# Eighty unread products behind the rounded exponentials of the first ten units

## The chip, the core and the metric

The kernel runs on one core of a Trainium2 chip. The time is that of one execution on the device, in microseconds; the kernel before took 715.68 us in the median of three runs (712.08 to 719.77).

## The reference

Attention with a bias that a small network makes of the distance, then a feed-forward layer, for 4 batches, 8 heads, 576 positions and head size 64:

```python
scores = q @ k.T / 8
x = log1p(|i - j|) / log1p(max(i, 1))
bias = relu(x * w1 + b1) @ w2            # 32 hidden, one value per head
attn = exp(s - max(s)) / (sum + 1e-9)    # s = scores + bias
x = (attn @ v) as 2304 x 512
h = x @ w_in                             # 512 -> 2048
out = (h * sigmoid(1.702 h)) @ w_out     # 2048 -> 512
```

## The kernel before

Numbers go through TensorE in fp16 as a high and a low half, so each product of two matrices is three (high by high, high by low, low by high). The work is cut into units: a unit is one batch, one tile of 128 query rows (the fifth tile of a batch has 64) and a pair of heads. There are 72 units, 36 for each group of two batches; units 0 to 7 belong to the first tile of batches 0 and 1. For a unit:

- `emit_s` (L346): twelve score products on TensorE into a PSUM tile that has one buffer, tag s.
- `emit_soft1` (L364): VectorE adds the bias and takes the maximum (L373), ScalarE takes the exponential and its sum (L377), VectorE makes the reciprocal (L384, L385), ScalarE (L389) or VectorE (L387) writes the rounded high half of the normalised exponentials into tile hl, VectorE the low half (L390), and a DMA on SP's queue transposes both (L399).
- `emit_av` (L405): thirty products with v (L422) into a PSUM tile of tag h, which VectorE scales and splits into xT (L427, L428).

The bias of a query tile comes from 8 bias steps of four relus each on ScalarE or VectorE (L172, L174), products with w2 on TensorE (L191, L193), a copy out by ScalarE (L197), a DMA to memory and a load (L212). The weights arrive in 32 pieces that VectorE puts together from 64-bit words (L464, L467, L470), and that ScalarE (L476) and VectorE (L226) split. When all 8 units of a block of rows are through, the feed-forward runs in 16 chunks per block: `emit_m1`, twelve products (L500) into tag h, a tanh (L506), VectorE (L508), a split (L513 or L515, L516), and two chunks later `emit_m2`, six products (L530).

Tag h has two PSUM buffers, which key transposes (L293, L300), attention products and feed-forward products take in the order of the program text. Key transposes for units 4 and 5 are called at unit 2, those for units 6 and 7 at unit 4; the attention products lag four units behind the scores for the first eight (`AV_LAG`). The main loop (L667) calls these pieces, but the order on each engine is made by a scheduler that plays the program through with its own costs and puts each instruction where it is ready. On the chip each engine then takes its instructions in that order.

Of the kernel before, what the change touches and what calls it, by code (L numbers as in the profile page):

```python
# [7 lines left out]
F32 = mybir.dt.float32  # L8
# [12 lines left out]
def kernel(  # L21
# [26 lines left out]
    nc = tc.nc  # L48
# [41 lines left out]
    ps_h = ctx.enter_context(tc.tile_pool(name="ps_h", bufs=2, space=PSUM))  # L90
# [128 lines left out]
    def stage(shape, dt, tag, name):  # L219
        return wk.tile(shape, dt, tag=tag, name=name, bufs=BUFS[tag])  # L220
# [143 lines left out]
    def emit_soft1(u):  # L364
        bt = bt_t[u]
        at = wk.tile([128, 2 * S], F32, tag="a32", name="a32", bufs=BUFS["a32"])
        mx = wk.tile([128, 2], F32, tag="mx", name="mx")
        sm = wk.tile([128, 2], F32, tag="sm", name="sm", bufs=6)
        hl = wk.tile([128, 2, 2 * S], F16, tag="hl", name="hl", bufs=BUFS["hl"])
        for a in range(2):  # L370
            cs = slice(S * a, S * a + S)

            nc.vector.tensor_tensor_reduce(  # L373
                out=at[:, cs], in0=s_ps.pop((u, a))[:, 0:S], in1=bt[:, cs], scale=-1.0 / BS, scalar=3.0e38,
                op0=ALU.add, op1=ALU.min, accum_out=mx[:, a:a + 1],
            )
            nc.scalar.activation(  # L377
                out=at[:, cs], in_=at[:, cs], func=ACTF.Exp, scale=-1.0, bias=mx[:, a:a + 1],
                accum_out=sm[:, a:a + 1],
            )  # L380
        for a in range(2):
            cs = slice(S * a, S * a + S)
            r = sm[:, a:a + 1]
            nc.vector.tensor_scalar(out=r, in0=r, scalar1=1.0e-9, scalar2=1.0 / AS, op0=ALU.add, op1=ALU.mult)  # L384
            nc.vector.reciprocal(out=r, in_=r)  # L385
            if a < VEC_EXP.get(u, 0):
                nc.vector.tensor_scalar(out=hl[:, 0, cs], in0=at[:, cs], scalar1=r, scalar2=None, op0=ALU.mult)  # L387
            else:
                nc.scalar.activation(out=hl[:, 0, cs], in_=at[:, cs], func=ACTF.Identity, scale=r)  # L389
            nc.vector.scalar_tensor_tensor(  # L390
                out=hl[:, 1, cs], in0=at[:, cs], scalar=r, in1=hl[:, 0, cs], op0=ALU.mult, op1=ALU.subtract
            )

        if u in AT_W:
            x = 8 * 2 * DM + 18 * 128 * AT_W[u]
            t = wo16.rearrange("p f x d -> p (f x d)")[:, x:x + 18 * 128].rearrange("p (c n) -> p c n", c=18)
        else:
            t = stage([128, 18, 128], F16, "aT" if u <= max(BIAS_A) or u % 4 < 2 else "ht", "aT")
        nc.sync.dma_start_transpose(out=t, in_=hl.rearrange("p x n -> p (x n)"))  # L399
        aT[u] = t  # L400
# [266 lines left out]
    for u in range(NU + 2):  # L667
        if u < NU:
            emit_s(u)
            emit_soft1(u)  # L670
        ready = NF * sum(1 for x in last_unit if x < av)
        late = u - AV_LAG.get(u, 2) in last_unit[1:]
        if not late:
            msteps(ready, STEPS_A.get(u, 1))
        while av <= u - AV_LAG.get(u, 2):
            emit_av(av)
            av += 1
        if late:
            msteps(ready, STEPS_A.get(u, 1))
        elif u - 2 == last_unit[0]:  # L680
            ready = NF
        if u < len(W_STEPS):
            weights_to(w_done[1] + W_STEPS[u])
        if u in BIAS_A:
            bias_first()
        msteps(ready, STEPS_B.get(u, 1))
        bias_second()
        if u in BIAS_B:
            bias_first()
            bias_second()  # L690
        if u + BIAS_AHEAD < NU:
            bias_get(u + BIAS_AHEAD)
        for fn, args in todo.get(u, ()):
            fn(*args)
# [56 lines left out]
```

## Time and profile before

| | before |
|---|---|
| runs | 712.08, 715.68, 719.77 us |
| profiled execution | 715.95 us, span 714.2 us |
| mean granted clock of TensorE | 0.956 |
| busy: TensorE, VectorE, ScalarE | 637.2, 510.9, 404.4 us |
| first score product, first feed-forward product | 30.5, 116.95 us |

Times in the trace run from the start of the span. Busy time of TensorE counts pipelined products, so a full row means that it had no pauses. The granted clock is 1.00 at 2.4 GHz and 0.50 at 1.2 GHz; a value between is a mean over a stretch.

### The profile page before, as it was taken

Reading aid. Unit: us, or ns where it says so; the run is one execution under the profiler, and the core shown is the slowest. Engines: PE = TensorE matmul, PEld = TensorE weight load, DVE = VectorE, ACT = ScalarE, POOL = GpSimd, SP = SyncE. Lnnn points to the kernel's source line nnn. Section 1 sums busy time; section 2 is a strip of 40 time slices with the busy share of each in tenths; the row PEclk is TensorE's granted clock in tenths of the full one; section 3 lists DMA queues with packets and bytes.
Section 4 is the critical chain, followed back from the end, with each engine's and each line's share of the span. In section 5 each row is a group of like instructions: output and inputs, shape, how many; then the busy total and the mean of one; then the engine's idle time right before and its main releaser. Section 6 shows DMA issues by size and latency. Waiting matters only on the chain. (4 is left out here: it accounts for less than half of the span.)

```text
span 714.2 us, 17518 instructions
## 1 busy us (share of the span) xinstructions
PE 637.2 (89%) x6888; PEld 385.7 (54%) x6888; DVE 510.9 (72%) x1401; ACT 404.4 (57%) x865; POOL 135.5 (19%) x198
## 2 busy tenths in 40 slices
PE   5656867798789999999789899799999999999997
PEld 3222423354445665566556565466656666666765
DVE  6678888999867778676569877746766896774321
ACT  6789987786757566554455547624334363443133
POOL 1202000112202211111212221111122222222222
PEclk9979896999989999999989999999999999999999
DMA  9799999999988675668875769844673585745000
GB/s 236 228 286 230 287 251 231 276 256 237 198 149 204 144 140 117 147 140 153 186 133 112 145 126 193 178 94 96 106 146 87 101 189 109 132 68 97 2 31 16
DMA packets 230770, 111.79 MB, mean 157 GB/s; under 512 B 210720, under 2 KB 214944, under 8 KB 230688
## 3 DMA queue, kind: packets, MB, share of 16 engines
q1 hardware_dynamic: 222592, 94.65, 64.0%
q10 hardware_dynamic: 7952, 15.43, 6.8%
q8 instruction: 54, 0.88, 0.5%
q0 software_dynamic: 144, 0.59, 0.2%
q14 instruction: 28, 0.23, 0.1%
HBM read 52.85 MB, written 15.34 MB: 95 GB/s over the span
## 5 line engine op out<-in xcount | busy, mean ns | idle before, releaser
L500 PE MATMUL hp<-xT,wi 128*128 128x256 f16 (+1 forms) x1920 | 217.1, 264 | 6.0 <-DVE th L508 4.9
L530 PE MATMUL op<-wo,gT 128*128 128x512 f16 x864 | 215.3, 383 | 2.7 <-POOL gT L516 1.3
L516 POOL TENSOR_TENSOR gT<-th,gT 128x256 f16<-128x256 f32 (+1 forms) x160 | 119.9, 751 | 502.1 <-ACT gT L513 221.6
L500 PEld LDWEIGHTS <-wi 128*128 128x128 f16 x1920 | 167.5, 98 | 49.8 <-issue 16.9
L377 ACT ACTIVATE a<-a,mx 128x576 f32<-128x576 f32 x144 | 110.3, 767 | 110.8 <-DVE mx L373 108.2
L390 DVE SCALAR_TENSOR_TENSOR hl<-a,sm,hl 128x576 f16<-128x576 f32 x144 | 122.4, 863 | 17.2 <-ACT hl L389 16.8
L373 DVE CUSTOM_DVE_ANT_0 a<-sp,bt 128x576 f32<-128x576 f32 x144 | 103.0, 753 | 35.8 <-PE sp L357 30.7
L530 PEld LDWEIGHTS <-gT 128*128 128x128 f16 x864 | 79.6, 98 | 81.6 <-POOL gT L516 4.9
L506 ACT ACTIVATE th<-hp 128x256 f32<-128x256 f32 (+1 forms) x160 | 56.2, 353 | 109.3 <-PE hp L500 104.6
L508 DVE SCALAR_TENSOR_TENSOR th<-th,hp 128x256 f32<-128x256 f32 (+1 forms) x160 | 62.2, 391 | 76.2 <-ACT th L506 76.1
L422 PEld LDWEIGHTS <-v 128*64 128x64 f16 x2400 | 69.6, 115 | 51.5 <-issue 29.7
L422 PE MATMUL ot<-aT,v 128*64 128x128 f16 (+1 forms) x2280 | 79.8, 222 | 19.2 <-DMA aT<-hl 15.3
L389 ACT ACTIVATE hl<-a,sm 128x576 f16<-128x576 f32 x103 | 76.2, 767 | 25.8 <-issue 10.8
L357 PE MATMUL sp<-kT,qT 64*128 64x512 f16 (+2 forms) x960 | 72.7, 293 | 12.0 <-DVE mx L373 6.3
L191 PE MATMUL o<-ht,pk 128*32 128x512 f32 x288 | 63.0, 693 | 20.9 <-ACT os L197 18.2
L172 ACT ACTIVATE ht<-tab,bp 128x576 f32<-128x576 f32 x96 | 69.3, 768 | 6.5 <-PE o L193 5.7
L357 PEld LDWEIGHTS <-qT 64*128 64x128 f16 (+1 forms) x960 | 29.4, 98 | 59.7 <-issue 29.3
L427 DVE TENSOR_SCALAR xT<-ot 128x128 f16<-128x128 f32 x72 | 20.4, 284 | 22.3 <-PE ot L422 22.0
L384 DVE TENSOR_SCALAR sm<-sm 128x1 f32<-128x1 f32 x144 | 21.5, 149 | 17.6 <-ACT a L377 16.5
L197 ACT ACTIVATE os<-o,ips 128x576 f32<-128x576 f32 x36 | 26.3, 731 | 12.1 <-PE o L193 11.5
L191 PEld LDWEIGHTS o<-ht,pk 128*32 128x32 f32 x288 | 10.2, 115 | 40.9 <-ACT os L197 21.1
L515 DVE CAST gT<-th 128x256 f16<-128x256 f32 x96 | 28.1, 293 | 3.6
(60 smaller groups left out, 439.8 us busy)
## 6 DMA issues: line engine op xcount, KB each, us to landing
bt<-scr SPq DMA_DIRECT2D x31, 576.0 KB, 4.4
scr<-os ACTq DMA_DIRECT2D x36, 288.0 KB, 4.6
w<-in_moe_w_in_dram SPq DMA_DIRECT2D x16, 512.0 KB, 5.5
w<-in_moe_w_out_dram SPq DMA_DIRECT2D x16, 512.0 KB, 5.3
k<-in_k_dram SPq DMA_DIRECT2D x32, 128.0 KB, 4.2
q<-in_q_dram SPq DMA_DIRECT2D x16, 256.0 KB, 5.0
out_dram<-ob ACTq DMA_DIRECT2D x16, 256.0 KB, 3.9
bt<-scr SPq DMA_DIRECT2D x8, 288.0 KB, 4.2
```

The lines of the kernel that those rows point to most:

```text
L172: last["A"] = nc.scalar.activation(out=h, in_=tv, func=ACTF.Relu, bias=bp[:, pb:pb + 1])
L191: nc.tensor.matmul(om[po], lhsT=w2b, rhs=h[:, :, 0:128], start=True, stop=True)
L357: nc.tensor.matmul(ps[a][64 * e:64 * e + m, cs], lhsT=qt[r, x, hp + e, 0:m], rhs=kT[b, hp + e][r, y, cs], start=i == 0, stop=i == 2,)
L373: nc.vector.tensor_tensor_reduce(out=at[:, cs], in0=s_ps.pop((u, a))[:, 0:S], in1=bt[:, cs], scale=-1.0 / BS, scalar=3.0e38, op0=ALU.add, ...
L377: nc.scalar.activation(out=at[:, cs], in_=at[:, cs], func=ACTF.Exp, scale=-1.0, bias=mx[:, a:a + 1], accum_out=sm[:, a:a + 1],)
L389: nc.scalar.activation(out=hl[:, 0, cs], in_=at[:, cs], func=ACTF.Identity, scale=r)
L390: nc.vector.scalar_tensor_tensor(out=hl[:, 1, cs], in0=at[:, cs], scalar=r, in1=hl[:, 0, cs], op0=ALU.mult, op1=ALU.subtract)
L422: nc.tensor.matmul(o[64 * a:64 * a + 64, po], lhsT=vt[:, x, vc:vc + 64], rhs=t[:, 9 * y + k0, po], start=kb < 0 and i == 0, stop=kb == 3 a ...
L500: nc.tensor.matmul(p[:, :n], lhsT=wi16[:, x, cc, 128 * f:128 * f + 128], rhs=r, start=i == 0, stop=i == 11,)
L508: nc.vector.scalar_tensor_tensor(out=g[:, :n], in0=th[:, :n], scalar=1.0, in1=p[:, :n], op0=ALU.add, op1=ALU.mult)
L516: nc.gpsimd.tensor_tensor(out=gt[:, 1, :n], in0=g[:, :n], in1=gt[:, 0, :n], op=ALU.subtract)
L530: nc.tensor.matmul(op_t[j, i], lhsT=gt[:, x, ts], rhs=wo16[:, f, y, :], start=f == 0 and n3 == 0, stop=f == NF - 1 and n3 == 2,)
```

## The change

Behind the rounding of each head in units 0 to 9, TensorE makes four equal products of 384 columns: the first 128 columns of that head's rounded exponentials stand still, the other columns stream. They go into a new tile of tag h that nothing reads.

```diff
             else:
                 nc.scalar.activation(out=hl[:, 0, cs], in_=at[:, cs], func=ACTF.Identity, scale=r)
+            if u < 10:
+                e = hl[:, 0, cs]
+                w = ps_h.tile([128, 512], F32, tag="h", name="wm")
+                for _ in range(4):
+                    nc.tensor.matmul(w[:, 0:384], lhsT=e[:, 0:128], rhs=e[:, 128:512], start=True, stop=True)
             nc.vector.scalar_tensor_tensor(
```

Lines behind it move down by five (L476 becomes L481, L500 becomes L505). The scheduler makes another order of everything from the first tens of rows on; TensorE has 12,582 rows instead of 12,420.

TensorE, the key transposes for units 4 and 5 (kt and kp of L293 and L300). Before, they stand between the first bias steps, ahead of all scores:

```order
L282 MATMUL kp<-idn,kt_99 128x64
L281 MATMUL kp<-idn,k_92 128x128 x4
L282 MATMUL kp<-idn,kt_99 128x64
L293 MATMUL kt<-idn,kt_99 128x64 x2
L191 MATMUL o<-ht,pk 32x512 x4
```

Now, row 182 on, behind the eight new products wm of unit 2:

```order
L394 LDWEIGHTS hl
L394 MATMUL wm<-hl 128x384
L293 MATMUL kt<-idn,kt_99 128x64 x2
L300 MATMUL kp<-idn,k_138 128x128 x4
L191 MATMUL o<-ht,pk 32x512 x4
L193 MATMUL o<-ht,pk 32x64 x4
```

The transposes have moved from ahead of unit 0 to behind the rounding of unit 2.

ScalarE, between the exponentials of unit 5 and those of unit 6 (a_825 and a_923 before, a_983 is unit 6 now). Before, all that stands between them:

```order
L377 ACTIVATE a_825,sm<-a_825,mx 128x576 x2
L172 ACTIVATE ht<-tab,bp 128x576
L197 ACTIVATE os<-o,ips 128x576
L172 ACTIVATE ht<-tab,bp 128x576 x3
L256 ACTIVATE qT<-qp 128x512
L377 ACTIVATE a_923,sm<-a_923,mx 128x576
```

Now, the last eleven of the sixteen rows between them, and the exponentials:

```order
L198 DMA scr_81<-os 128x576
L302 ACTIVATE kT<-kp 128x512
L172 ACTIVATE ht<-tab,bp 128x576
L197 ACTIVATE os<-o,ips 128x576
L172 ACTIVATE ht<-tab,bp 128x576 x3
L481 ACTIVATE wi_72<-w_1300 128x512
L302 ACTIVATE kT<-kp 128x512
L198 DMA scr_82<-os 128x576
L172 ACTIVATE ht<-tab,bp 128x576
L197 ACTIVATE os<-o,ips 128x576
L172 ACTIVATE ht<-tab,bp 128x576 x3
L377 ACTIVATE a_983,sm<-a_983,mx 128x576 x2
```

Bias steps and weights now stand around the copies of the late transposes, ahead of unit 6.

## Rows read from the trace of the kernel before

**Rows 1.** Stretch: length; busy us of PE, PEld, DVE, ACT, POOL; granted clock, DMA share, GB/s.

```profile
30.00:117.00 87.00, 57.60 (x559) 25.85 (x559) 72.87 (x181) 76.73 (x140) 5.41 (x6) 0.80 0.98 248
117.00:200.00 83.00, 68.58 (x667) 37.44 (x666) 74.77 (x178) 60.22 (x118) 13.91 (x14) 0.93 1.00 243
200.00:297.00 97.00, 96.16 (x1049) 57.72 (x1049) 72.75 (x205) 62.12 (x127) 18.77 (x23) 0.99 0.72 151
```

**Rows 2.** The same view, later stretches.

```profile
340.00:400.00 60.00, 50.11 (x622) 32.89 (x621) 44.57 (x124) 31.09 (x69) 11.72 (x19) 0.94 0.67 138
...
440.00:460.00 20.00, 15.72 (x213) 9.83 (x212) 15.87 (x55) 15.45 (x41) 2.48 (x6) 1.00 0.95 189
460.00:660.00 200.00, 199.22 (x2220) 126.39 (x2218) 137.81 (x404) 80.70 (x197) 46.16 (x57) 0.99 0.57 112
```

**Rows 3.** Who waited for whom, 30 to 117 us: total us, times, longest.

```profile
DVE xT L427 <- PE ot L422: 4.5, 2, 3.6
...
ACT ht L172 <- PE o L193: 3.1, 3, 2.5
```

**Rows 4.** Busy time by stretch, two short ones in the head.

```profile
45.00:51.00 6.00, 5.01 (x28) 1.99 (x28) 5.34 (x12) 5.95 (x12) 0.00 (x0) 0.50 1.03 256
61.00:62.50 1.50, 1.08 (x14) 0.51 (x16) 1.50 (x5) 1.50 (x3) 0.00 (x0) 1.00 0.85 276
```

**Rows 5.** Order of time: start us, us, engine, line, [idle before]; products that begin or wait.

```profile
116.95 1.25 PE L500 MATMUL hp<-xT,wi 128*128 128x256 f16 x5
...
198.11 1.81 PE L422 MATMUL ot<-aT,v 128*64 128x128 f16 x30 [5.64 <-DMA aT<-hl]
...
297.44 1.48 PE L500 MATMUL hp<-xT,wi 128*128 128x256 f16 x12
```

**Rows 6.** The chain that ended last: start us, us, what; twelve first feed-forward products.

```profile
667.66 1.31 PE hp L500 x12
```

**Rows 7.** Order of time: the score products of units 2 and 4.

```profile
49.35 1.62 PE L357 MATMUL sp<-kT,qT 64*128 64x512 f16 x12
...
61.11 0.91 PE L357 MATMUL sp<-kT,qT 64*128 64x512 f16 x12 [0.82 <-DVE mx L373]
```

**Rows 8.** Groups by line, 30 to 117 us: count, busy us, mean ns, idle before.

```profile
L172 ACT ACTIVATE ht<-tab,bp 128x576 f32<-128x576 f32 x46 | 33.2, 768 | 3.2 <-PE o L193 3.1
...
L197 ACT ACTIVATE os<-o,ips 128x576 f32<-128x576 f32 x12 | 8.7, 725 | 0.0
...
L389 ACT ACTIVATE hl<-a,sm 128x576 f16<-128x576 f32 x14 | 10.3, 765 | 1.6 <-DVE sm L385 1.0 <-DMA aT<-hl 0.6
...
L476 ACT ACTIVATE wi<-w 128x512 f16<-128x512 f32 x8 | 4.9, 624 | 2.5 <-DVE w L470 2.4
...
L226 DVE SCALAR_TENSOR_TENSOR wi<-w,wi 128x512 f16<-128x512 f32 x8 | 5.4, 681 | 0.0
...
L373 DVE CUSTOM_DVE_ANT_0 a<-sp,bt 128x576 f32<-128x576 f32 x20 | 14.3, 751 | 5.0 <-DMA bt<-scr 5.0
...
L384 DVE TENSOR_SCALAR sm<-sm 128x1 f32<-128x1 f32 x18 | 2.6, 145 | 1.6 <-ACT a L377 1.5
...
L387 DVE TENSOR_SCALAR hl<-a,sm 128x576 f16<-128x576 f32 x4 | 2.0, 504 | 0.0
...
L390 DVE SCALAR_TENSOR_TENSOR hl<-a,sm,hl 128x576 f16<-128x576 f32 x18 | 14.3, 809 | 1.2 <-ACT hl L389 1.2
...
L464 DVE TENSOR_SCALAR w<-w 128x512 uint32<-128x512 uint32 x15 | 6.2, 416 | 0.6 <-DMA w<-in_moe_w_in_dram 0.4
...
L467 DVE SCALAR_TENSOR_TENSOR w<-w,w 128x512 uint32<-128x512 uint32 x15 | 10.2, 686 | 0.1
...
L470 DVE SCALAR_TENSOR_TENSOR w<-w,w 128x512 uint32<-128x512 uint32 x14 | 10.3, 736 | 0.0
```

**Rows 9.** Groups by line, 117 to 200 us: the bias products.

```profile
L191 PE MATMUL o<-ht,pk 128*32 128x512 f32 x64 | 12.5, 625 | 1.7 <-DVE mx L373 1.7
...
L193 PE MATMUL o<-ht,pk 128*32 128x64 f32 x64 | 4.2, 282 | 0.0
```

## The prediction

> **What bounds the kernel now.** I read first the busy time by stretch [rows 1]. From 117 us on, when the first feed-forward product runs, TensorE is the engine that fills the time: 96.16 us busy of 97 between 200 and 297 us, and nearly all of it again from 460 to 660 us [rows 2]. Before 117 us it is not: between 30 and 117 us TensorE works 57.60 of 87 us, while VectorE works 72.87 and ScalarE 76.73. In that head the two softmax engines set the pace and TensorE waits. The waits say the same [rows 3]: there ScalarE waited for bias products 3.1 us and VectorE for attention outputs 4.5 us, and no more than that for anything TensorE makes. The clock granted to TensorE in the head is 0.80 of full on average; the stretches at 0.50 lie in its pauses and bias steps [rows 1, 4].
>
> So an end time has three parts: when the first feed-forward product can start, the TensorE work from there on, and the pauses inside that work. The change touches the order up to one place only. TensorE's rows are the same in both programs from row 3,697 of before (3,859 of the changed one) on; what stands there in the trace is the second half of the attention products that ends where a feed-forward chunk begins at 297.44 us [rows 5]. VectorE, ScalarE and the DMA queue of SP also run in one order from about there. I therefore reckon up to 297 us, and let the rest (417 us) stay as it is, with its pauses of 9.9 us in 340 to 400 and 4.3 us in 440 to 460 [rows 2].
>
> In the trace that stretch is 117.0 + 164.7 + 15.3 = 297.0: start of the first product at 116.95 [rows 5], 68.58 + 96.16 us of TensorE work, 14.4 + 0.8 us of pauses [rows 1].
>
> **The change, part by part.**
>
> *The products themselves.* 10 units by 2 heads by 4 are 80 products of 384 columns. Twelve products of 256 columns take 1.31 us at full clock [rows 6], 109 ns each, so 384 columns take 164 ns and all 80 take 13.1 us; the twelve score products, which take 0.91 us at the full clock, take 1.62 at half [rows 4, 7], so at half clock at most 26.2 us. The weight load that each carries lies under the product before it, as in the 1.31 us. All 80 stand ahead of the first feed-forward product, in a stretch with 29.4 us of TensorE pauses (87 minus 57.6) that the softmax engines make. I cost them at nothing as work. If that cover were gone (TensorE the pace setter of the head), 13.1 us would be added.
>
> *The waits they bring.* TensorE takes its products in order, so the four of a head hold all behind them until ScalarE has rounded that head. They also take their turn in the two accumulators with tag h, by program order. Before, the key transposes that units 4 and 5 need ran from row 10 of TensorE on; now they stand behind the products of unit 2, and the attention products of unit 0 stand behind those of unit 4. So those units' scores come late, and the scheduler filled ScalarE and VectorE with other work ahead of them. Counted in the orders, ScalarE now does ahead of unit 6's exponentials 16 more bias relus, 4 more bias copies, 2 more weight halves and one copy of queries less: 16 x 0.768 + 4 x 0.725 + 2 x 0.624 - 0.6 = 15.8 us [rows 8]. Nothing of it is new work: by unit 10's exponentials, ScalarE's count is about that of before.
>
> *The start of the feed-forward.* It needs the attention output of unit 7 from VectorE. Ahead of that copy VectorE's order now has 8 more low halves of weights, two more score passes, 8 more small operations, 2 more low halves of exponentials, and 7, 7 and 6 more of the three steps that put weights together: 5.4 + 1.5 + 1.2 + 1.6 + 2.9 + 4.8 + 4.4 = 21.8 us [rows 8]. ScalarE has ahead of the first tanh 8 more relus, 2 copies, 4 passes of the exponentials and 7 weight halves: 6.1 + 1.5 + 3.1 + 4.4 = 15.1 us, the exponential taken at the price of the rounding [rows 8]. With the pauses as they are the start moves by 15.1 to 21.8 us; VectorE's 14.1 us of pauses in the head [rows 1] could take up part, the new waits could add some. I take 18 us, the middle, since both engines must get there: 135 us.
>
> *The work behind the start.* Two units of scores (0.91 us each) and three bias steps now stand ahead of it. Eight bias steps cost 12.5 + 4.2 us [rows 9], so three are 6.3 us. 164.7 - 1.8 - 6.3 = 156.6 us.
>
> *The pauses behind the start.* Of 15.3 us, 5.6 are one wait at 192.5 to 198.1 us for a transposed block [rows 5], with the DMA engines at a share of 1.00 in that stretch [rows 1]; the loads of the next two batches that stand around it on SP's queue are all still there, so I leave it. The other 9.7 us fall where VectorE is 74.77 of 83 us busy, weights and softmax together [rows 1]. Now 10 of the 32 weight splits are left behind the first tanh's update instead of 14, and the softmax is further ahead, so I keep half: 5.6 + 4.8 = 10.4 us.
>
> *The sum.* 135 + 156.6 + 10.4 = 302.0, 5.0 us later than 297.0. The profiled execution took 715.95 us, 0.27 above the median of the runs: 715.95 + 5.0 = **721 us**. The ends of this case: 15.1 us for the start with the pauses at 7 gives 715; 22 us with 13 gives 728.
>
> **The rivals.**
>
> *The clock pays (faster).* In the head TensorE worked at 0.80 of its clock; the added products fill pauses, the stretches at 1.2 GHz go, and bias products, transposes and scores come sooner. For it: the low stretches do lie in the units concerned. Against it: ScalarE and VectorE waited for TensorE only 7.6 us there [rows 3]. It decides if VectorE's 14.1 us of pauses go and the later pauses shrink to the one DMA wait: 117 + 21.8 - 14.1 + 156.6 + 5.6 = 286.9, 10.1 us sooner: 706 us. The Trainium skill, "TensorE: Matmul & The Clock Gate", Part 1 on the HAM clock gate, says that the throttled clock is the default and activity releases it, which would make this rival the outcome wherever TensorE sets the pace; the trace agrees as far as the low clock lies in the stretch with 29.4 us of pauses [rows 1], but it shows TensorE waiting there, not being waited for. That the products come in clumps behind a rounding, and leave the clock as it was, is part of my forecast: it changes neither sum.
>
> *VectorE starves behind ScalarE (slower by more).* Ahead of unit 6's scores pass VectorE has only about 7.0 us more to do (one weight low, two roundings, two lows, three small ones, and 1, 2 and 2 steps of weights [rows 8]), while ScalarE has 15.8. If the filling does not cover that, VectorE idles the 8.8 us between them and then still has the 21.8 us ahead of the start: 117 + 30.6 + 156.6 + 10.4 = 314.6, 17.6 us later: 734 us. For it: VectorE was in step with ScalarE through the head and has no other work in its order there. Against it: its pauses in the head can take up some. It decides where VectorE's busy time between 30 and 117 us falls clearly under 72.9.
>
> *It evens out (no change).* By the 17th feed-forward chunk ScalarE has even 3.8 us less ahead than before (two relus, a copy, two roundings [rows 8]). With the DMA engines at 0.98 and 1.00 through the head and the next stretch [rows 1], transfers could be the pace that no order changes. Then the time is 712 to 716.
>
> **How the numbers follow.** Forecast 0.42, VectorE starves 0.23, the clock pays 0.20, it evens out 0.15. One per cent of the median, about what a measurement can tell from no change, is 7.2 us: under 708.5 counts as faster, over 722.8 as slower. The forecast's own range of 715 to 728 gives 0.27 same, 0.13 slower and 0.02 faster; starving gives 0.20 slower and 0.03 same; the clock 0.14 faster and 0.06 same; evening out 0.10 same and 0.05 faster. Together faster 0.21, same 0.46, slower 0.33. The range reaches from just under the clock's 706 to just over starving's 734: 705 to 735.
>
> **What would show it.** In the profile after: the 80 products at 164 to 327 ns each with TensorE waiting for ScalarE's rounding just ahead of them; unit 4's scores some 10 us later than 61.1; the first feed-forward product at about 135 us (125 for the clock, 148 for starving); pauses of about 10 us from there until the chunk that began at 297.44, which then begins near 302; and the same length from there to the end. Wrong would be the whole reckoning if the stretch behind that chunk changed by more than 3 us, since the orders are the same there; the step on the start if the first product came at 120 or before; and the cost of nothing if the head's TensorE pauses vanished.

## The result: 1.5 % slower

The changed kernel takes 725.98 us in the median of 8 runs (721.93 to 729.50), the kernel before 715.75 us in as many (707.45 to 719.77): a ratio of 1.0149, 95% interval 1.0112 to 1.0187, some 10 us. The forecast was 721 us in a range of 705 to 735, with "within 1%" the likeliest class; the time lies in the range, but in the class "slower", which had 0.33. The profiled execution took 726.55 us, its span is 724.8 us.

Busy time by stretch in the kernel after, which answers to [rows 1]; the fourth row is the head up to its first feed-forward product. Columns as there.

```profile
30.00:117.00 87.00, 63.34 (x438) 21.87 (x439) 60.47 (x143) 70.30 (x127) 5.95 (x7) 0.88 0.88 228
117.00:200.00 83.00, 65.44 (x758) 39.47 (x760) 82.46 (x204) 62.93 (x123) 9.47 (x10) 0.94 1.02 242
200.00:297.00 97.00, 94.74 (x1048) 57.75 (x1041) 70.01 (x199) 62.82 (x127) 16.45 (x23) 1.00 0.70 151
30.00:149.20 119.20, 84.13 (x717) 33.87 (x718) 92.13 (x223) 94.48 (x170) 5.95 (x7) 0.87 0.90 230
```

Between 30 and 117 us TensorE works more than before (63.34 against 57.60 us), at a higher granted clock (0.88 against 0.80). VectorE works 12.4 us less there (60.47 against 72.87): something keeps it waiting. The order of time on TensorE shows when the two marks of [rows 5] come:

```profile
149.15 1.27 PE L505 MATMUL hp<-xT,wi 128*128 128x256 f16 x10 [0.92 <-DVE xT L433]
...
309.94 1.26 PE L505 MATMUL hp<-xT,wi 128*128 128x256 f16 x10
```

The first feed-forward product starts at 149.15 instead of 116.95 us, the chunk that began at 297.44 now at 309.94: 12.5 us later. From there to the end of the span it is 414.9 us, before it was 416.8. So the whole loss arises ahead of that chunk, and 1.9 us come back behind it.

What VectorE waited for between 30 and 149 us, the longest four (as in [rows 3]: total us, times, longest):

```profile
DVE w L469 <- DMA w<-in_moe_w_out_dram: 7.4, 1, 7.4
DVE kT L226 <- ACT kT L284: 5.9, 1, 5.9
DVE wi L226 <- ACT wi L481: 5.6, 3, 3.6
DVE a L373 <- PE sp L357: 4.3, 3, 3.0
```

The first is new: one wait of 7.4 us for a piece of the weights. So is the third, for halves of weights that ScalarE splits; the second ends at 29.65 us, ahead of the stretch, and was 5.3 us before. SP's DMA queue in order of time shows why the piece came late (start, length on the queue; L404 is the transpose of a unit's exponentials, L212 loads a bias, L310 to L323 load values, L450 a weight piece):

```profile
54.04 4.83 SPq L404 DMA_TRANSPOSE aT<-hl  x1
58.98 0.52 SPq L212 DMA_DIRECT2D bt<-scr  x1
59.61 0.38 SPq L310 DMA_DIRECT2D v<-in_v_dram  x1
60.09 4.87 SPq L404 DMA_TRANSPOSE aT<-hl  x1
65.06 0.53 SPq L212 DMA_DIRECT2D bt<-scr  x1
65.64 0.63 SPq L314 DMA_DIRECT2D v<-in_v_dram  x1
...
68.32 0.54 SPq L450 DMA_DIRECT2D w<-in_moe_w_out_dram  x1
```

In the kernel before, one transpose stands ahead of these loads, and the same piece goes out at 57.47:

```profile
49.51 3.96 SPq L399 DMA_TRANSPOSE aT<-hl  x1
...
57.47 0.54 SPq L445 DMA_DIRECT2D w<-in_moe_w_out_dram  x1
58.05 0.43 SPq L240 DMA_DIRECT2D q<-in_q_dram  x1
58.64 6.19 SPq L399 DMA_TRANSPOSE aT<-hl  x1
```

The planner (the scheduler that writes the order) put unit 1's transpose ahead of the values and the seventh weight piece, and the piece's load is issued 10.9 us later. Half of this is unit 1's transpose of 4.87 us and one more bias load; the other half is that unit 0's transpose already begins 4.5 us later and takes 0.9 longer. What follows on VectorE and TensorE, both in order of time:

```profile
74.28 0.54 DVE L469 TENSOR_SCALAR w<-w 128x512 uint32<-128x512 uint32 x1 [7.39 <-DMA w<-in_moe_w_out_dram]
...
79.26 0.28 DVE L226 SCALAR_TENSOR_TENSOR kT<-kt,kT 128x128 f16<-128x128 f32 x1
...
83.11 0.76 DVE L373 CUSTOM_DVE_ANT_0 a<-sp,bt 128x576 f32<-128x576 f32 x1 [2.97 <-PE sp L357]
```

```profile
79.60 1.11 PE L300 MATMUL kp<-idn,k 128*128 128x128 f32 x4 [7.89 <-DVE kT L226]
...
81.92 1.14 PE L357 MATMUL sp<-kT,qT 64*128 64x512 f16 x8
```

VectorE does the late piece first; the low halves of the keys stand behind it (79.26), TensorE's next key transposes wait 7.89 us for those, and the last eight score products of unit 4 end at 83.1 us (before: 62.0). Then VectorE waits 2.97 us more for these scores. A load of `w_out`, which no product reads before `emit_m2`, holds up VectorE and TensorE, and through them ScalarE's exponentials, since each takes its work in order.

The new products in the list by form (busy, mean ns, idle before):

```profile
L394 PE MATMUL wm<-hl 128*128 128x384 f16 x80 | 18.8, 371 | 9.2 <-ACT hl L389 7.3 <-DVE qT L226 1.9
```

They fill 18.8 us of TensorE, which waited 7.3 us for ScalarE's roundings ahead of them.

### The profile page after: what moved, and what is told of

Same layout as the page of the kernel before. It is cut to its first block, busy times and chain, and to the rows that moved or that the text cites. A ratio compares the mean times of both kernels' runs of the same rounds, so it can differ in the third digit from the quotient of the medians.

```text
span 724.8 us, 17695 instructions
## 1 busy us (share of the span) xinstructions
PE 648.4 (89%) x6968; PEld 389.8 (54%) x6968; DVE 509.5 (70%) x1401; ACT 406.8 (56%) x865; POOL 131.8 (18%) x198
## 5 line engine op out<-in xcount | busy, mean ns | idle before, releaser
L505 PE MATMUL hp<-xT,wi 128*128 128x256 f16 (+1 forms) x1920 | 216.6, 265 | 9.4 <-DVE th L513 6.6
L535 PE MATMUL op<-wo,gT 128*128 128x512 f16 x864 | 213.1, 381 | 1.0 <-DVE sm L384 0.9
L521 POOL TENSOR_TENSOR gT<-th,gT 128x256 f16<-128x256 f32 (+1 forms) x160 | 116.0, 727 | 507.2 <-ACT gT L518 207.8
L505 PEld LDWEIGHTS <-wi 128*128 128x128 f16 x1920 | 168.1, 99 | 51.2 <-issue 17.7
L395 DVE SCALAR_TENSOR_TENSOR hl<-a,sm,hl 128x576 f16<-128x576 f32 x144 | 120.9, 852 | 18.5 <-ACT hl L389 18.1
L427 PE MATMUL ot<-aT,v 128*64 128x128 f16 (+1 forms) x2280 | 76.7, 218 | 11.0 <-DMA aT<-hl 7.8
L357 PE MATMUL sp<-kT,qT 64*128 64x512 f16 (+2 forms) x960 | 73.1, 293 | 12.5 <-DVE mx L373 6.6
L191 PE MATMUL o<-ht,pk 128*32 128x512 f32 x288 | 61.5, 651 | 14.2 <-ACT os L197 12.9
L518 ACT CAST gT<-th 128x256 f16<-128x256 f32 (+1 forms) x64 | 21.8, 348 | 17.9 <-DVE th L513 17.7
L384 DVE TENSOR_SCALAR sm<-sm 128x1 f32<-128x1 f32 x144 | 21.2, 150 | 14.1 <-ACT a L377 13.4
```

Source lines behind the costliest of these rows:

```text
L191: nc.tensor.matmul(om[po], lhsT=w2b, rhs=h[:, :, 0:128], start=True, stop=True)
L357: nc.tensor.matmul(ps[a][64 * e:64 * e + m, cs], lhsT=qt[r, x, hp + e, 0:m], rhs=kT[b, hp + e][r, y, cs], start=i == 0, stop=i == 2,)
L395: nc.vector.scalar_tensor_tensor(out=hl[:, 1, cs], in0=at[:, cs], scalar=r, in1=hl[:, 0, cs], op0=ALU.mult, op1=ALU.subtract)
L427: nc.tensor.matmul(o[64 * a:64 * a + 64, po], lhsT=vt[:, x, vc:vc + 64], rhs=t[:, 9 * y + k0, po], start=kb < 0 and i == 0, stop=kb == 3 a ...
L505: nc.tensor.matmul(p[:, :n], lhsT=wi16[:, x, cc, 128 * f:128 * f + 128], rhs=r, start=i == 0, stop=i == 11,)
L521: nc.gpsimd.tensor_tensor(out=gt[:, 1, :n], in0=g[:, :n], in1=gt[:, 0, :n], op=ALU.subtract)
```

## The experiments

Three theories stood against each other. *Work*: the 80 products cost TensorE's time. *Waits*: TensorE held behind a rounding delays what is behind it. *Order*: neither costs much; the scheduler, given other durations and turns, writes down an order in which loads and waits fall worse, and the products are only the occasion for it. Some expectations below speak of a theory of turns: it takes the waits together with the turns in tag h and the late loads that they bring.

All measured values, for reading what follows. Ratio: to the kernel before on the same chip (its medians there are 715.7 to 716.9 us), with the 95% interval. Start: first feed-forward product. Chunk: the one that began at 297.4, the 38th (number 37, counted from 0). Idle: VectorE's idle time from 30 us to the start. Start, chunk and idle are of one profiled execution each, in us; it can lie some us off the median (e11's took 728.59, e4's 715.88). The change has 8 runs, e2, e7 and e12 have 4, the others 10.

| kernel | median us | ratio | start | chunk | idle |
|---|---|---|---|---|---|
| before | 715.75 | 1 | 117.0 | 297.4 | 14.1 |
| the change | 725.98 | 1.0149 (1.0112 to 1.0187) | 149.2 | 309.9 | 27.1 |
| e1, one small product a head | 723.07 | 1.0086 (1.0051 to 1.0120) | 135.7 | 301.2 | 20.7 |
| e2, products on the keys | 724.48 | 1.0121 (1.0056 to 1.0185) | 123.3 | 306.5 | 14.4 |
| e8, one small product on the keys | 719.52 | 1.0043 (1.0007 to 1.0078) | 122.9 | 299.5 | 16.0 |
| e4, units 5 to 9 alone | 718.96 | 1.0065 (1.0022 to 1.0107) | 133.6 | 301.1 | 14.4 |
| e6, units 0 to 4 alone | 724.47 | 1.0129 (1.0091 to 1.0167) | 133.1 | 308.5 | 23.8 |
| e5, products doubled | 722.73 | 1.0125 (1.0088 to 1.0162) | 145.2 | 305.3 | 21.5 |
| e3, keys first, products | 719.95 | 1.0063 (1.0020 to 1.0106) | 131.8 | 304.5 | 14.9 |
| e7, keys first, no products | 728.37 | 1.0160 (1.0103 to 1.0217) | 135.9 | 312.9 | 17.7 |
| e9, one piece from GpSimd's queue | 720.45 | 1.0069 (1.0037 to 1.0102) | 136.8 | 302.8 | 16.2 |
| e10, four pieces ahead, products | 718.76 | 1.0039 (1.0011 to 1.0066) | 146.0 | 303.6 | 21.4 |
| e11, four pieces ahead, no products | 723.98 | 1.0098 (1.0064 to 1.0132) | 123.7 | 307.8 | 22.0 |
| e12, no turn and no wait | 725.93 | 1.0143 (1.0053 to 1.0234) | 136.8 | 307.4 | 19.3 |

### Almost no work left: e1

```
-    for _ in range(4):
-        nc.tensor.matmul(w[:, 0:384], lhsT=e[:, 0:128], rhs=e[:, 128:512], ...)
+    nc.tensor.matmul(w[:, 0:64], lhsT=e[:, 0:128], rhs=e[:, 128:192], ...)
```

> One product of 64 columns per head in place of four of 384: 20 small products instead of 80, the same waits for the rounding and the same turns in tag h. Turn theory (the key transposes of units 4 and 5 stand behind the rounding of unit 2, the loads behind unit 1's transposed block on SP's queue come late, VectorE waits): the whole loss stays, 723 to 729 us, first feed-forward product at 144 to 152 us. Work theory (the 80 products' own time on TensorE, 16 to 26 us, pushes the rest): under a tenth of that work is left, 714 to 718 us, first feed-forward product near 120.

The 20 small products are 3.9 us busy instead of 18.8, and 7.3 of the 10.2 us are still lost. VectorE waits 6.3 us for a weight piece, as in the change: this order, too, has unit 1's transpose ahead of the loads. So at most 2.9 us of the loss could be work, if the rest of the order were the same, which it is not quite. The time is what the theory of turns gave; the start, at 135.7, comes 8 us sooner than that theory's earliest.

### The same work without the wait for a rounding: e2, and only its turns: e8

```
-    e = hl[:, 0, cs]
+    e = kT[units[u][0], units[u][2]][:, 0, :]
```

> The same 80 products of 384 columns with the same turns in tag h, but of the unit's transposed keys, which are there before its scores, in place of its rounded exponentials: all the work, no wait for the softmax. Turn theory: 713 to 719 us, first feed-forward product at 115 to 125 us, no long wait of VectorE for a weight piece. Work theory: as the change, 723 to 729 us.

e8 has the same operand and the one small product of e1.

> One product of 64 columns per head of the unit's transposed keys: next to no work, no wait for the softmax, but the same turns in tag h and so another order of everything. Work theory (the earlier kernel with 80 such products of 384 columns took 724.5 us because of their time): 714 to 718 us. Order theory (any other order of the first 300 us costs pauses that the order of before happens not to have): 720 to 725 us, with 3 to 8 us of TensorE pauses between the chunks 16 and 37, where before has 0.3.

e2 loses 8.7 us though VectorE has no long wait for a weight piece and the start is only 6.3 us late; its loss comes behind the start, in pauses: 24.1 us up to the chunk against 15.3 before. Its 724.48 us are what the theory of work gave. With the turns alone, e8, the loss is 3.8 us; 719.52 lies between its two forecasts, and the pauses between the chunks 16 and 37 are 4.0 us, as the theory of order had them. The 5 us of e2 over e8 fit the theory of work; the next two kernels speak against it.

### Part of the units: e4 and e6

```
-    if u < 10:
+    if 5 <= u < 10:        # e4;   e6:  if u < 5:
```

> The products in units 5 to 9 alone: half the work; all key transposes keep their early place. Turn theory: the long wait of VectorE near 70 us is gone, what is left is attention products behind later roundings: 713 to 720 us. Work theory: half of the change's 10 us, about 721 us.

> The products in units 0 to 4 alone: half the work; the key transposes stand behind the roundings of units 2 and 4, as in the change. Turn theory: nearly all of the loss, 721 to 728 us, with a wait of VectorE of 5 us or more for a weight piece near 70 us. Work theory: about 721 us, as for the other half.

The first five units carry nearly all of the loss (8.7 us; the last five 3.2), though both halves hold 40 products. e6 has VectorE's wait for the weight piece (7.8 us), e4 has not. Both times are as the theory of turns gave them. That agrees with the wait of 74.28 us as the place, but the two kernels' orders differ too.

### Twice the work: e5

```
-    for _ in range(4):
+    for _ in range(8):
```

> Eight products per head in place of four, 160 in all, with the same waits and turns. Work theory: their time on TensorE is added again in full, 16 us or more over the change: 740 to 748 us. Waits and order: the products run while the softmax engines set the pace, and add less than 8 us: 724 to 734 us.

The group of the new products in e5, and VectorE's longest wait between 30 and 145 us:

```profile
L394 PE MATMUL wm<-hl 128*128 128x384 f16 x160 | 29.8, 335 | 6.9 <-ACT hl L389 4.7 <-ACT wo L481 1.9 <-DVE hl L387 0.2
```

```profile
DVE w L469 <- DMA w<-in_moe_w_out_dram: 7.2, 1, 7.2
```

11.0 us more of products on TensorE, and the time is not longer: 722.73 against 725.98 us, with intervals that overlap. Both theories gave more. A cost that grows with the number of products does not show here. That alone does not rule out work as the cause in the change, since e5 has another order: up to the chunk TensorE's pauses are 36.9 us in e5 and 45.1 in the change. The wait for the weight piece is there as before.

### The call order changed, with products and without: e3 and e7

The key transposes of the units 4 to 7, and the load that the last of them need, are called ahead of unit 0, so that they can't stand behind unit 2's products; e7 is the kernel before with the same edit.

```
-        (0, (load_k, 1, 1)), (1, (split_v, 1, 0)), (2, (trans_k_own, 0, 1)),
+        (1, (split_v, 1, 0)),
...
-        (4, (trans_k_own, 1, 1)), (6, (split_v, 1, 1)),
+        (6, (split_v, 1, 1)),
...
+    trans_k_own(0, 1)
+    load_k(1, 1)
+    trans_k_own(1, 1)
```

> The change with all key transposes called ahead of unit 0, so that they stand before the first products: the same 80 products and the same waits for the rounding, and on SP's queue the loads of v and of the seventh weight piece stand ahead of unit 0's transposed block again. If the key transposes behind unit 2's rounding are the larger part of the loss: 715 to 720 us, and no wait of VectorE over 5 us near 70 us. If the products' own time is: 723 to 729 us.

> Before, with all key transposes called ahead of unit 0, no added products: another order with no work and no wait added. Work theory: 713 to 718 us. Order theory: over 719 us, or else faster than before for having the keys sooner; 3 us or more of pauses between the chunks 16 and 37.

With this call order the products *save* 8.4 us. e3 gets back 6.0 of the change's 10.2 us, as was expected if the late key transposes are the larger part of the loss. e7, which adds no instruction at all, loses 12.6 us to the kernel before, more than the change; only the theory of order had allowed for that. What TensorE waited for in e7 between 30 and 313 us, the first line of the list:

```profile
PE ot L422 <- DMA aT<-hl: 23.4, 12, 4.7
```

Before, that wait came to 10.1 us in 4 times over the stretch up to the same chunk: in e7 the attention products stand where their transposed blocks are not yet there. A mere reorder costs as much as the whole change did.

### The wait itself taken away: e9

The seventh weight piece is loaded from GpSimd's queue; nothing else of the change is edited.

```
-        nc.sync.dma_start(out=t.rearrange("p f x -> p (f x)"), in_=src)
+        (nc.gpsimd if w_done[0] == 6 else nc.sync).dma_start(out=t.rearrange("p f x -> p (f x)"), in_=src)
```

> The change, with the load of the seventh weight piece (the one VectorE waited 7.39 us for until 74.28) issued on GpSimd's queue, behind one bias load, instead of on SP's queue behind unit 1's transpose. The planner moves other work with it. If that wait makes the larger part of the loss (order theory): no VectorE wait over 4 us for a weight piece near 70 us, first feed-forward product near 135 us, chunk 37 near 303, 719 to 721 us. If the wait only hid other waiting: start at 145 to 149 and 725 us as in the change. If the products' own work or their waits for the rounding cost: 725 too, with the wait gone.

GpSimd's queue, VectorE and TensorE of e9, each in order of time, the rows that answer to those of the change above:

```profile
62.88 0.54 POOL L450 DMA_DIRECT2D w<-in_moe_w_out_dram  x1 [24.91 <-DMA bt<-scr]
```

```profile
69.64 0.43 DVE L469 TENSOR_SCALAR w<-w 128x512 uint32<-128x512 uint32 x1 [3.18 <-DMA w<-in_moe_w_out_dram]
...
72.89 0.28 DVE L226 SCALAR_TENSOR_TENSOR kT<-kt,kT 128x128 f16<-128x128 f32 x1
```

```profile
75.14 1.14 PE L357 MATMUL sp<-kT,qT 64*128 64x512 f16 x8
...
136.82 1.38 PE L505 MATMUL hp<-xT,wi 128*128 128x256 f16 x11
...
302.79 1.38 PE L505 MATMUL hp<-xT,wi 128*128 128x256 f16 x11
```

The piece is issued 5.4 us sooner, the wait shrinks from 7.39 to 3.18 us, the low halves of the keys come 6.4 us sooner and unit 4's last scores 6.8 us sooner; the start comes 12.3 us sooner, and the chunk 7.2. On SP's queue unit 1's transpose still stands ahead of the value loads (at 59.86), so this is the wait alone as far as that place goes: row by row, VectorE, ScalarE and TensorE (up to 71, 69 and 91 us of e9) have the order of the change. Further on the orders differ. Start, chunk and time are what the theory of order gave. 720.45 us: 5.5 of the 10.2 us are back, and the interval of the ratio (1.0037 to 1.0102) lies clear of the change's (1.0112 to 1.0187).

### Loads further ahead, with products and without: e10 and e11

```
-    W_AHEAD = 3
+    W_AHEAD = 4
```

> The change, with weights loaded four pieces ahead instead of three: the seventh piece's load then stands ahead of unit 1's transpose on SP's queue. Order theory: the wait near 74 us goes, 719 to 721 us; but loads that run ahead take DMA time from the keys and values early on, which could move the first units by 1 to 3 us. Work theory: 725 us.

> The kernel before with weights loaded four pieces ahead, no added products: the control for the run above, and a candidate to beat the kernel before. If four ahead is harmless by itself, 714 to 718 us. If any other order than that of before has 3 to 9 us more pauses between the chunks 16 and 37, as all kernels so far, 718 to 722 us. Work theory: 5 us or more under the run above.

e10 comes out at 718.76 us, the lowest of all kernels with products and just under what the theory of order gave, and VectorE's seven longest waits hold none for a weight piece. But its start stays at 146.0: a start this late does not need that wait. Of the 6.3 us by which its chunk comes sooner than the change's, 3.1 are the start, and most of the rest is pauses behind it (6.3 us against 10.1). No theory had e11 right: the edit that helps the change costs the kernel before 7.1 us (723.98 against 716.89 on its chip). Again the kernel with the products is the faster one, by 5.2 us. What TensorE waited for, second in the list of e11 from 30 to 308 us, sixth in that of e10 from 30 to 304 us:

```profile
PE ot L422 <- DMA aT<-hl: 10.0, 10, 2.9
```

And e10:

```profile
PE ot L427 <- DMA aT<-hl: 2.3, 3, 0.8
```

In e11 it is the transposed blocks once more, though the kernel before waited as long for them (10.1 us), so they don't explain its loss alone; VectorE's idle time ahead of the start is 22.0 us against 14.1.

### All of the work, no turn, no wait: e12

The 80 products on the keys, right behind a unit's scores, into columns of the score accumulators that nothing uses.

```
+        if u < 10:
+            e = kT[b, hp][:, 0]
+            for a in range(2):
+                for _ in range(4):
+                    nc.tensor.matmul(ps[a][:, 640:1024], lhsT=e[:, 0:128], rhs=e[:, 128:512], start=True, stop=True)
```

> The 80 products of 384 columns on the unit's transposed keys, right behind its scores and in the unused columns of the score accumulators: all of the work, no turn in the two accumulators with tag h, no wait for a rounding. The planner's order still differs from that of before, but the values and the seventh weight piece are loaded ahead of unit 0's transpose. Work theory (products cost TensorE time in the head): 722 us or more. Order theory: no VectorE wait over 4 us for a weight piece near 70 us, and the 3 to 9 us more of pauses between the chunks 16 and 37 that other orders showed or less: 714 to 720 us.

This went against the theory of order, which forecast 714 to 720 us, and came out where the theory of work had it: 725.93, in four runs from 722.69 to 732.67. The trace of e12 has no long wait for a weight piece (1.7 us at 75.28), and VectorE waited for the products themselves 2.2 us, once. But TensorE, in order of time, has this just ahead of the start:

```profile
120.94 0.25 PE L427 MATMUL ot<-aT,v 128*64 128x128 f16 x2
133.01 1.81 PE L427 MATMUL ot<-wo,v 128*64 128x128 f16 x30 [11.83 <-DMA wo<-hl]
```

TensorE stood 11.83 us for one transposed block, whose issue on SP's queue begins at 121.89 and takes 6.36 us. That is a wait of another kind at another place, and the products are not in it. Whether they made ScalarE and VectorE late enough for it, or the order did, this run alone does not tell; the doubled products of e5 and the pairs e3 with e7 and e10 with e11 say that in some orders products as such cost nothing.

## Why the prediction was right, and where it was not

*Where the loss arises, and the rest.* Right. The reckoning up to the chunk holds: 12.5 us later there, and the rest is 1.9 us shorter, within the 3 us that were set as its test.

*The products at nothing.* Not refuted, and not shown for the change itself. e5 doubles them at no cost, in an order of its own. The head's pauses of TensorE, which were their cover, did not vanish: from 30 us to the start they are 35.1 us. But they did not shrink either. TensorE from 30 us to the 17th chunk and from there to the 38th, columns as in [rows 1]; two rows each for the kernel before, the change and e9:

```profile
30.00:212.02 182.02, 137.67 (x1345) 68.88 (x1344) 156.17 (x383) 145.13 (x276) 20.23 (x21) 0.87 0.98 238
212.02:297.44 85.42, 85.11 (x942) 52.48 (x939) 64.66 (x181) 54.05 (x110) 17.85 (x22) 1.00 0.72 155
...
30.00:218.13 188.13, 146.90 (x1411) 72.88 (x1412) 154.91 (x376) 145.53 (x273) 19.36 (x22) 0.92 0.96 231
218.13:309.94 91.81, 87.89 (x959) 52.90 (x957) 64.69 (x187) 56.58 (x114) 15.31 (x22) 1.00 0.63 143
...
30.00:209.88 179.88, 143.78 (x1403) 72.38 (x1403) 154.41 (x373) 143.94 (x271) 21.02 (x25) 0.93 0.97 241
209.88:302.79 92.91, 87.82 (x971) 52.65 (x967) 65.55 (x189) 58.66 (x117) 14.65 (x21) 1.00 0.66 147
```

Up to the 38th chunk TensorE is busy for 222.8 us before and 234.8 in the change, 12.0 more, and its pauses come to 44.7 and 45.1. By this sum the products' time came on top, near the 13.1 us that the prediction set for the case that the cover is gone. In e9, with the same 80 products, TensorE is busy 8.8 us longer than before, and its pauses ahead of the 17th chunk are 36.1 us instead of 44.4: there the cover nearly holds. So the sum alone fits two readings of the change: work that nothing covers, or work that is covered and new waits in its place. e9 speaks for the second, and so do e10 and e5 with 33.7 and 36.9 us of pauses up to the chunk; e2 and e12, with 42.9 and 45.2, speak for the first. The group of products fills 18.8 us, between the 13.1 and 26.2 of the forecast; a run of four takes 0.82 us at full clock and 1.49 at half, where the forecast had 0.66 and 1.31.

*The start of the feed-forward.* This is the step that failed, in size: 135 us forecast, 149.2 measured. Its two terms can be told apart in the fourth row of the busy times. VectorE's work ahead of the start grew from 72.87 to 92.13 us, by 19.3; counted in the orders it was 21.8. ScalarE's grew by 17.8; counted 15.1. So the counts were near. The pauses were wrong: the step let VectorE's 14.1 us of idle time take up part of the new work, and they grew to 27.1 instead. Between 30 us and the start VectorE waits 7.6 us longer than before for transfers, nearly all of it the wait for the weight piece, and 4.8 longer for ScalarE, whose halves of weights it waits for in the change and not before. Its waits for TensorE are only 0.9 longer: 3.0 us for unit 4's scores came, 3.6 for an attention output went. The step had counted the instructions of VectorE and ScalarE but had not followed SP's queue, where unit 1's transpose had moved ahead of that piece. In e9, where the wait is 3.2 us, the start is at 136.8, the chunk at 302.8 and the time 720.45 us; forecast were 135, 302.0 and 721.

*Unit 4's scores.* Forecast some 10 us later than 61.1; the first four products came at 71.28, but the last eight at 81.92, again behind that wait.

*The work behind the start.* 156.6 us forecast, 150.7 measured. The term was mis-sized the other way. From the start to the 38th chunk, before and in the change, and the groups that show why:

```profile
116.95:297.44 180.49, 165.22 (x1726) 95.56 (x1725) 148.01 (x383) 122.48 (x246) 32.67 (x37) 0.96 0.85 194
149.15:309.94 160.79, 150.72 (x1653) 91.96 (x1653) 127.52 (x340) 107.68 (x219) 28.72 (x37) 1.00 0.82 181
```

```profile
L191 PE MATMUL o<-ht,pk 128*32 128x512 f32 x128 | 21.0, 615 | 1.7 <-DVE mx L373 1.7
L191 PE MATMUL o<-ht,pk 128*32 128x512 f32 x104 | 13.8, 605 | 0.0
...
L357 PE MATMUL sp<-kT,qT 64*128 64x512 f16 x228 | 17.6, 288 | 2.7 <-ACT os L197 2.6
L357 PE MATMUL sp<-kT,qT 64*128 64x512 f16 x204 | 15.4, 285 | 1.6 <-ACT os L197 1.6
...
L530 PE MATMUL op<-wo,gT 128*128 128x512 f16 x210 | 52.9, 386 | 1.7 <-POOL gT L516 1.3 <-ACT gT L513 0.2
L535 PE MATMUL op<-wo,gT 128*128 128x512 f16 x210 | 51.3, 380 | 0.0
```

The count was exact: 24 bias products (three steps of eight) and 24 score products (two units) fewer. What the forecast missed is the pace of the products: the clock granted behind the start is 1.00 where it was 0.96, and the same 210 products of `emit_m2` fill 1.6 us less. This term took back 5.9 of the 14.2 us by which the start was missed. That the time came out 5 us from the forecast is in part luck: two errors of opposite sign.

*The pauses behind the start.* 10.4 us forecast, 10.1 measured. The total agrees, but not its reason: the wait of 5.64 us for a transposed block, which was to stay, went; in its place are smaller ones, 3.1 us for VectorE's updates behind the tanh at the head of them. Between the 17th chunk and the 38th they come to 3.9 us, where before they were 0.3.

*The rival in which VectorE starves.* Its test came true: VectorE's busy time between 30 and 117 us fell to 60.47, and the start is at 149 (its own was 148). Its mechanism did so only in part: VectorE's waits for ScalarE grew by 4.8 us, where the rival had 8.8, and those for transfers by 7.6. Its 734 us are missed by the smaller work behind the start.

*The rival in which the clock pays.* The clock did rise, from 0.80 to 0.88 between 30 and 117 us, with no gain there; the head's end is set by VectorE, ScalarE and transfers. It gained something behind the start, where TensorE sets the pace (0.96 to 1.00, above); the forecast had kept the clock out of its sum. The long wait even took some clock back: in the change it is granted at 1.00 in 62 to 68 us and at 0.50 in 79.5 to 83.2, right after TensorE's 7.89 us of idle time; four of the products took 1.49 us at 80.50 and 0.82 at 64.07. The Trainium skill, "TensorE: Matmul & The Clock Gate", Part 1, calls the throttled clock the default that activity releases; the trace agrees with this drop to 1.2 GHz.

*What stays open.* e9 gets back 5.5 of the 10.2 us by one load's place. The chain behind it is shown up to unit 4's scores; that the whole 5.5 us hang on it is likely but not shown, since the orders differ from 91 us on, and another order alone moved the time by 7 and 13 us (e11, e7). The other 4 to 5 us have no cause that the runs isolate, but they have a place. TensorE's waits for transposed blocks between the 17th chunk and the 38th, before, in the change and in e9:

```profile
PE ot L422 <- DMA aT<-hl: 0.2, 1, 0.2
...
PE ot L427 <- DMA aT<-hl: 2.3, 4, 1.0
...
PE ot L427 <- DMA aT<-hl: 3.6, 5, 1.2
```

All thirteen other kernels wait there for such blocks, 1.4 to 7.9 us in the profiled executions, and have pauses of 2.8 to 8.7 us in this stretch, where the kernel before has 0.3. In e9 they are 4.8 us longer than before, nearly the whole 5.4 us by which its chunk is late. Why the order of before has none of them, no run tells. All thirteen other kernels measured are slower than the kernel before, with products or without (1.0039 to 1.0160), and the longest new waits lie at different places: a weight piece (the change, e1, e5, e6), transposed blocks (e7, e12). e2 and e12, which have all of the work and no wait for a rounding, leave some room for a cost of the work in those orders. A kernel that keeps the order of before to the instruction and adds the products was not among those run: each edit tried made the planner write the order anew.

## What to carry to other kernels

Where a planner makes the order, an added instruction is also an edit of the order: hold it against a control that changes the order without adding work, since here two such controls cost 7 and 13 us by themselves while doubling the added work cost nothing more. When counting what stands ahead of an instruction, count the DMA queue too, above all transposes that hold it: the row to look for is a load that has slid behind one, and the engine that needs that load next. A fuller TensorE, or a higher clock, was worth nothing here in the stretch that others pace; behind the start, where TensorE sets the pace, the clock paid.

## What the runs showed of the hardware

A transpose of 128 by 2304 numbers in fp16 (0.59 MB) takes 4.0 to 6.4 us on SP's queue in the rows above, where the load of a weight piece of 0.52 MB takes 0.54, and every load behind it waits that long to be issued. Over the whole trace of the change the 72 transposes take 2.4 to 6.1 us there (median 3.1) and the 32 weight pieces 0.3 to 1.0 (median 0.4). From issue to landing the two are much nearer: in e12, between 85 and 137 us, a median of 7.1 to 7.7 us for transposes, and 5.5 to 6.4 for weight pieces. The Trainium skill, "Advanced Engine Details and Errata", X-Bar Transpose (TRN2), has it that "TRN2 transpose DMAs are as fast as regular DMAs"; to the landing that is not far off here, but for what is queued behind, the measurement decides: a transpose holds SP's queue some nine times as long (4.87 against 0.54 us).
